# Three output products moved from the last steps of an attention kernel into its closing chain

## The chip, the cores and the metric

The kernel runs on one core of a Trainium2 chip. The metric is the device time of one execution in microseconds (us); the number of record is the median of several executions. The engines are named as in the profile: PE is TensorE (matmuls, with its weight loads listed apart as PEld), DVE is VectorE, ACT is ScalarE, POOL is GpSimd, and SP is SyncE, whose queue issues nearly all transfers (DMAs).

## What is computed

Two branches over the same `x` of 2048 tokens and 512 features are mixed by a gate:

```
g = sigmoid((x * gate_w).sum(-1))
a = softmax(q k^T / 4) v, 32 heads of 16, then @ wo      # q, k, v from x @ wqkv
b = x, with two routed tokens (the top 2 of x @ w_r) updated by a SwiGLU FFN
out = g * a + (1 - g) * b
```

## The kernel before

**Units and steps.** The attention is cut into 32 units; a unit is a pair of heads over half the queries, and the last four units (28 to 31) each take four heads over a quarter of the queries. A unit has 16 steps, one for each tile of 128 keys, so there are 512 steps. In a step `s`, `s_piece` (L634) makes four score tiles of 128x512 on PE (L641) and ACT takes their exponentials (L642) into `P`. Three of the four score tiles come from the PSUM pool `st` (3 buffers), and near the end one comes from `mxb` (1 buffer). `av_mm` (L644, L650) multiplies the exponentials with `V`, which has a column of ones, so that the sums of the softmax come out with the output; it runs two steps behind the scores. While units are left, a third stream, `m_piece` (L563, L573, L577), finds row maxima on PE and DVE; it has ended by the stretch that matters here.

**The order is written by hand.** The Python program's order is each engine's order. In the last steps a step is: four score matmuls, then `p_v(s - 2)` (the sums of two steps earlier), then one piece of the generator `slots()` (L800), then what `at_step` has registered for the step.

**The output projection.** `acc` holds 16 tiles of 128 tokens by 512 features, preloaded with `(1 - g) * b`. The features of heads 0 to 23 are projected through `wo` earlier, by `wo_part` and `acc_add` (L458: ACT scales the PSUM tile by `g` into a new tile `w`, L461, and POOL adds it to `acc`, L462). The last eight heads (feature group 3) come at the end: `split_last` (L528) splits a quarter of the queries into a rounded high part and a low rest, and `wo_last(t, 128)` (L551) does tile `t`: three matmuls (high x high, low x high, high x low; L495, in the PSUM tile `fl`), `finish` (L544: one DVE instruction, L546, `acc + g * product`) and `store` (L548, a DMA of 256 KB on SP's queue, L549). `slots()` places these for `t` = 0 to 11, one in each step: 0 to 3 from step 478 on, 4 to 7 from step 494 on, 8 to 11 from step 505 on (L846 to L850). Tiles 9, 10 and 11 therefore stand in steps 506, 507 and 508. The split halves that they read, `lastp[1]`, have been written by then.

**The closing chain.** Tiles 12 to 15 need the last unit, so they come in `tail()` (L733) after the last step, as a chain: ACT copies the sums out of PSUM (L663); PE picks the softmax sums (L739); DVE takes reciprocals (L741); ACT and DVE spread them (L744, L745); PE transposes the spread (L748) into `mxb` and `fl`; DVE multiplies (L751); ACT and DVE split into high and low (L69, L70); PE makes the four output products, three matmuls each (L758); DVE finishes each (L546) and SP stores it (L549).

## Time and profile before

| | us |
|---|---|
| median of 3 runs | 1437.01 (1435.02 to 1437.27) |
| time of the profiled execution | 1437.04 |
| its span, first to last instruction | 1435.2 |
| PE / DVE / ACT / POOL busy in the span | 1423.6 / 1295.4 / 1169.7 / 312.0 |

In the views of the profile, an entry of the timeline gives its start in the span, its length, the engine, the line and what is written from what; `x3` merges three instructions. Matmuls overlap their successors, so the length of one contains some of the next. The table by stretches of time gives for each engine the busy time and in brackets the number of instructions, and then the clock granted to TensorE as a share of full speed, the mean busy share of the 16 DMA engines (it can come out a little over 1) and GB/s. The chain of waits is followed back from the last instruction.

### The profile page before, as it was taken

What the parts mean: (1) busy time and instruction counts of PE and PEld (TensorE: products, weight loads), DVE (VectorE), ACT (ScalarE), POOL (GpSimd) and SP (SyncE); (2) the same over time, 40 slices, a digit from 0 to 9 for tenths busy, and PEclk for the clock granted to TensorE, in tenths of its full rate; (3) what the DMA queues carried; (4) which work ended last, traced back from release to release, by engine and by line L of the source; (5) the groups of instructions that cost most, each with busy time, mean ns of one, the idle gap of its engine ahead of it and who ended that gap; (6) DMA issues with size and microseconds to landing.
All of it is one profiled execution on the core that took longest, in us unless ns stands there. A gap on an engine that the chain in (4) does not pass through costs nothing.

```text
span 1435.2 us, 24154 instructions
## 1 busy us (share of the span) xinstructions
PE 1423.6 (99%) x9113; PEld 630.2 (44%) x9113; DVE 1295.4 (90%) x1535; ACT 1169.7 (82%) x2262; POOL 312.0 (22%) x328
## 2 busy tenths in 40 slices
PE   9999999999999999999999999999999999999998
PEld 6654444444444444444444444344444444444433
DVE  5879999999999999999999999999999999999942
ACT  4568888888888888888888888888888888888885
POOL 3652000112000001200000100032742322234500
PEclk9999999999999999999999999999999999999998
DMA  8612021212214121312222332414313031012012
GB/s 266 185 33 63 20 53 31 53 45 40 54 50 112 62 53 30 68 29 57 65 82 53 87 87 73 108 41 128 82 31 68 23 75 37 13 30 58 16 50 77
DMA packets 55096, 92.87 MB, mean 65 GB/s; under 512 B 14208, under 2 KB 25472, under 8 KB 53476
## 3 DMA queue, kind: packets, MB, share of 16 engines
q1 hardware_dynamic: 54884, 91.32, 24.3%
q8 instruction: 72, 1.18, 0.4%
q14 instruction: 44, 0.36, 0.1%
q0 software_dynamic: 96, 0.01, 0.0%
HBM read 63.77 MB, written 28.57 MB: 64 GB/s over the span
## 4 chain that ended last, share of the span: by engine, by line
PE 96%; DMA 2%; DVE 1%; ACT 0%; SPq 0%; issue 0%; ACTq 0%; DVEq 0%
PE av L650 35%; PE st L641 23%; PE mxa L573 12%; PE mxb L573 10%; PE fl L153 6%; PE fl L495 4%; PE st L282 3%; DMA xs<-xT 1%; PE mxa L600 1%; DMA wvs<-wqkv 1%; PE fl L386 0%; PE st L153 0%; DVE Mr L577 0%; DMA k_scr<-Qx 0%; ACT P L642 0%; PE fl L424 0%
## 5 line engine op out<-in xcount | busy, mean ns | idle before, releaser
L642 ACT ACTIVATE P<-st 128x512 f32<-128x512 f32 x2028 | 1064.5, 599 | 204.2 <-PE st L641 102.3
L577 DVE TENSOR_REDUCE Mr<-mxa 128x2 f32<-128x1024 f32 x655 | 794.4, 1213 | 4.0 <-PE mxa L573 3.5
L650 PE MATMUL av<-P,V 128*32 128x512 f32 x4096 | 545.3, 604 | 0.0
L641 PE MATMUL st<-Qx,Kx 50*128 50x512 f32 x2028 | 537.8, 443 | 1.8 <-ACT P L642 1.7
L577 DVE TENSOR_REDUCE Mr<-mxb 128x1 f32<-128x512 f32 x654 | 451.8, 691 | 63.5 <-PE st L641 18.6
L641 PEld LDWEIGHTS st<-Qx,Kx 50*128 50x128 f32 x2028 | 275.3, 184 | 232.7 <-ACT P L642 213.0
L573 PE MATMUL mxb<-Kx,Qx 48*128 48x512 f32 x654 | 325.4, 498 | 0.0
L573 PE MATMUL mxa<-Kx,Qx 48*128 48x512 f32 x1310 | 296.9, 420 | 1.2 <-DVE Mr L577 1.2
L573 PEld LDWEIGHTS mxb<-Kx,Qx 48*128 48x128 f32 x654 | 119.5, 183 | 273.7 <-DVE Mr L577 251.9
L573 PEld LDWEIGHTS mxa<-Kx,Qx 48*128 48x128 f32 x1310 | 124.9, 183 | 52.1 <-DVE Mr L577 9.9
L650 PEld LDWEIGHTS av<-P,V 128*32 128x32 f32 x4096 | 81.1, 108 | 140.6 <-issue 134.5
L189 POOL TENSOR_SCALAR ev<-pe 128x512 fp32r<-128x512 f32 x24 | 35.7, 1489 | 321.5 <-ACT pe L187 321.5
L76 POOL TENSOR_SCALAR hl<-m 128x16 fp32r<-128x16 f32 x32 | 8.1, 254 | 440.0 <-DVE m L616 440.0
L462 POOL TENSOR_TENSOR acc<-acc,w 128x512 f32<-128x512 f32 x32 | 41.0, 1280 | 166.9 <-ACT w L461 152.8
L153 PE MATMUL fl<-xh,wh 128*128 128x512 f32 x96 | 42.9, 447 | 0.0
L153 PE MATMUL fl<-xh,wl 128*128 128x512 f32 x96 | 40.4, 420 | 0.0
L546 DVE SCALAR_TENSOR_TENSOR acc<-fl,gg,acc 128x512 f32<-128x512 f32 x16 | 12.0, 748 | 26.3 <-PE fl L495 24.0
L495 PE MATMUL fl<-woh,ahl 128*128 128x512 f32 x96 | 35.2, 447 | 0.0
L605 DVE TENSOR_REDUCE Mr<-mxa 128x2 f32<-128x1024 f32 x21 | 25.7, 1222 | 8.3 <-PE mxa L600 8.3
L153 PE MATMUL fl<-xl,wh 128*128 128x512 f32 x96 | 32.6, 421 | 0.0
L190 POOL TENSOR_TENSOR ev<-pe,ev 128x512 fp32r<-128x512 f32 x24 | 30.8, 1283 | 2.0
L282 PE MATMUL st<-Kx,xh 128*128 128x512 f32 x64 | 28.1, 440 | 0.0
(173 smaller groups left out, 763.0 us busy)
## 6 DMA issues: line engine op xcount, KB each, us to landing
Kx<-k_scr SPq DMA_DIRECT2D x30, 256.0 KB
k_scr<-ev SPq DMA_DIRECT2D x14, 512.0 KB
q_scr<-ev SPq DMA_DIRECT2D x14, 512.0 KB
Qx<-q_scr SPq DMA_DIRECT2D x54, 128.0 KB
Qx<-q_scr SPq DMA_DIRECT2D x70, 64.0 KB
xs<-xT SPq DMA_DIRECT2D x16, 256.0 KB
xn<-x SPq DMA_DIRECT2D x4, 1024.0 KB
Qx<-hr SPq DMA_DIRECT2D x256, 2.0 KB
```

The costliest lines, as they stand in the source:

```text
L153: nc.tensor.matmul(ps, a[:, i, c, :], b[nb][:, c, :], start=n == 0, stop=n == 11)
L189: nc.gpsimd.tensor_scalar(ev[:, 0], t, 1.0, None, op0=OP.mult)
L190: nc.gpsimd.tensor_sub(ev[:, 1], t, ev[:, 0].bitcast(F32))
L282: nc.tensor.matmul(ps, a[nb][:, c, sl], b[:, c, :], start=c == 0 and n == 0, stop=c == 3 and n == 2)
L462: nc.gpsimd.tensor_add(a, a, w)
L495: nc.tensor.matmul(ps, a[:, sl], b[:a.shape[0], c, :], start=first and n == 0, stop=last and n == 2)
L573: nc.tensor.matmul(dst, Qx[u % 3][64 * j:64 * j + 48, t * 128:t * 128 + 128], k_of(u, t // 4)[64 * j:64 * j + 48, c * 512:c * 512 + 512], ...
L577: nc.vector.tensor_reduce(Mr[:, g0:g0 + (2 if r == 1 else 1)], MX[r - 1], axis=AX.X, op=OP.max, negate=True)
L605: nc.vector.tensor_reduce(*r, axis=AX.X, op=OP.max, negate=True)
L641: nc.tensor.matmul(ps, k, q, start=True, stop=True)
L642: nc.scalar.activation(P[s][:, 2 * j + c, :], ps, AF.Exp)
L650: nc.tensor.matmul(AV[0][32 * ct:32 * ct + 32, :], V[:, kt, h * VW:h * VW + 32], P[s][:, ct, :], start=kt == 0, stop=kt == KT - 1)
```

## The change

The loop in `slots()` now ends with tile 8, so steps 506, 507 and 508 no longer have an output product. Tiles 9, 10 and 11 are done in `tail()` by a new helper `late_wo(i)`, which makes the same three matmuls for tile 10 (`i` = 0), 11 (1) and 9 (2), into the two banks of `mxa` and into a tile of `st`. Tile 10 stands ahead of the pick of the sums and keeps its finish on DVE. Tile 11 stands after the spreading of the reciprocals, tile 9 after the split; both are finished by `acc_add`, on ACT and POOL. Each store follows its finish in SP's queue. The second bank of the last four products is now `av` in place of `mxa`.

```diff
 def tail():
     ps = st_tile((128, 16))
+    pw = mxa_tile()
+    pw = pw[:, 0], pw[:, 1], st_tile()
+
+    def late_wo(i):
+        wo_terms(pw[i], *lastp[1], 3, slice((2 + i if i < 2 else 1) * 128, (3 + i if i < 2 else 2) * 128), True, True)
+
+    late_wo(0)
+    finish(10, pw[0])
+    store(10)
     for c in range(4):
         nc.tensor.matmul(ps[:, 4 * c:4 * c + 4], o[:, c * 128:c * 128 + 128], sel_l, start=True, stop=True)
...
     nc.scalar.activation(rx[:, 0:8], rb[:, 0:8], AF.Copy)
     nc.vector.tensor_copy(rx[:, 8:16], rb[:, 8:16])
+    late_wo(1)
+    acc_add(11, pw[1], gg)
+    store(11)
     pr = [mxb_tile((128, 256)), fl_tile((128, 256))]
...
         split(hl[0][:, sl], hl[1][:, sl], o[:, sl])
-    banks = [st_tile(), mxa_tile()[:, 0], st_tile(), mxb_tile()]
+    late_wo(2)
+    acc_add(9, pw[2], gg)
+    store(9)
+    banks = [st_tile(), av_tile(), st_tile(), mxb_tile()]
...
-        for t in range(12):
+        for t in range(9):
             if t % 4 == 0:
                 yield from wait((478, 494, 505)[t // 4])
             wo_last(t, 128)
```

## The prediction

> **What bounds the kernel now.** I read the page first, then the chain of waits, then the timeline of the last 40 us.

> ```profile
> PE 1423.6 (99%) x9113; PEld 630.2 (44%) x9113; DVE 1295.4 (90%) x1535; ACT 1169.7 (82%) x2262; POOL 312.0 (22%) x328
> PE 96%; DMA 2%; DVE 1%; ACT 0%; SPq 0%; issue 0%; ACTq 0%; DVEq 0%
> ```

> PE carries the chain nearly to the end, so the change can act in two places only: the three steps that lose work, and the closing chain, where PE waits for others. The steps, in the chain (start, length) and then in the timeline:

> ```profile
> 1410.21 0.91 PE fl L495 x3
> 1411.12 0.66 PE st L641 x3
> 1411.78 1.00 PE av L650 x8
> ```

> ```profile
> 1399.01 0.73 PE L641 MATMUL st<-Qx,Kx 50*128 50x512 f32 x3
> 1400.67 1.00 PE L641 MATMUL st<-Qx,Kx 50*128 50x512 f32 x3
> 1403.08 0.73 PE L641 MATMUL st<-Qx,Kx 50*128 50x512 f32 x3
> 1405.04 0.73 PE L495 MATMUL fl<-woh,lahl 128*128 128x512 f32 x2
> 1405.93 0.50 PE L641 MATMUL st<-Qx,Kx 50*128 50x512 f32 x2
> 1413.61 0.73 PE L641 MATMUL st<-Qx,Kx 50*128 50x512 f32 x3
> 1418.65 2.78 PE L650 MATMUL av<-P,V 128*32 128x512 f32 x24
> ```

> A step with an output product is PE end to end: 0.91 + 0.66 + 1.00 = 2.57 us. Steps 503, 504 and 505 (scores from 1399.01) had none before tile 8's product at 1405.04: 6.03 us for three, 2.01 each. There ACT shares the bound:

> ```profile
> 1399.54 1.58 ACT L642 ACTIVATE P<-st 128x512 f32<-128x512 f32 x3 [0.50 <-PE st L641]
> 1401.46 1.61 ACT L642 ACTIVATE P<-st 128x512 f32<-128x512 f32 x3
> 1402.89 0.67 ACT L642 ACTIVATE P<-mxb 128x512 f32<-128x512 f32 x1
> 1403.62 1.57 ACT L642 ACTIVATE P<-st 128x512 f32<-128x512 f32 x3
> ```

> Four exponentials took 1.92 us from 1399.54 and 2.16 from 1401.46. The sums end at E = 1418.65 + 2.78 = 1421.43. From E on:

> ```profile
> 1422.15 1.05 PE L739 MATMUL st<-cst,o 128*128 128x4 f32 x8 [0.72 <-ACT o L663]
> 1423.24 0.26 DVE L741 RECIPROCAL rl<-st 128x16 f32<-128x16 f32 x1 [8.77 <-PE st L739]
> 1423.59 0.41 ACT L744 ACTIVATE rxl<-rl 128x256 f32<-128x256 f32 x1 [1.50 <-DVE rl L741]
> 1424.06 1.22 PE L748 MATMUL mxb<-cst,rxl 128*128 128x128 f32 x4 [0.86 <-ACT rxl L744]
> 1425.08 1.06 PE L748 MATMUL fl<-cst,rxl 128*128 128x128 f32 x4
> 1425.39 0.42 DVE L751 TENSOR_TENSOR o<-o,mxb 128x256 f32<-128x256 f32 x1 [1.51 <-PE mxb L748]
> 1426.37 0.79 PE L758 MATMUL st<-wz,onh 128*128 128x512 f32 x1 [0.23 <-ACT onh L69]
> 1428.86 0.63 PE L758 MATMUL mxa<-wz,onh 128*128 128x512 f32 x1
> 1429.28 0.63 PE L758 MATMUL st<-wz,onh 128*128 128x512 f32 x1
> 1431.46 0.75 DVE L546 SCALAR_TENSOR_TENSOR acc<-mxb,gg,acc 128x512 f32<-128x512 f32 x1
> ```

> PE waits 0.72, then 0.86, then 0.23 us. Its matmuls are slow too: L758's start 0.42 us apart (1428.86, 1429.28), where L495's three take 0.91 together. The granted clock says why (third number from the right; all but the first are stretches of one width, and within the first the clock halves at 27.69):

> ```profile
> 27.50:28.00 0.50, 0.50 (x3) 0.45 (x2) 0.00 (x0) 0.00 (x0) 0.50 (x1) 0.69 1.02 221
> 24.28:27.69 3.41, 1.93 (x7) 1.03 (x7) 2.45 (x3) 1.57 (x4) 2.75 (x2) 1.00 0.89 224
> 31.10:34.51 3.41, 3.01 (x13) 1.79 (x12) 3.41 (x5) 0.60 (x1) 0.00 (x0) 1.00 0.88 227
> 1420.34:1423.75 3.41, 2.15 (x20) 1.15 (x15) 0.42 (x2) 0.75 (x2) 0.00 (x0) 1.00 0.00 0
> 1423.75:1427.16 3.41, 2.87 (x10) 2.25 (x11) 1.39 (x5) 1.09 (x3) 0.00 (x0) 0.50 0.00 0
> 1427.16:1430.57 3.41, 3.41 (x9) 2.67 (x10) 1.85 (x3) 0.00 (x0) 0.00 (x0) 0.50 0.20 76
> ```

> From 1423.75 to 1430.57 PE has half its clock, 6.82 us. The stretch before had PE busy 2.15 of 3.41 us; 1.93 of 3.41 was followed by half clock as well (from 27.69 on), 3.01 was not. At half clock, 2.87 did not bring full clock back and 3.41 did.

> **The sum, part by part.** All times below are of this execution: 1437.04 us, which is its span of 1435.2 plus 1.84, and 0.03 over the median of the runs.

> *Steps 506 to 508.* Removed: nine matmuls, three finishes, three stores. The scores of 506 start at 1405.93 as before. Steps 503 to 505 are the pattern for what follows: 1405.93 + 6.03 = 1411.96 for the scores of 509, against 1413.61. For 510 and 511 I go on with the two limits seen, PE in order and four exponentials in 1.92 to 2.16 us: 2.14 and 1.96, so scores of 511 at 1416.06, where they were at 1417.69; the last sums, 24 records, then run 1417.18 to 1419.96. Taken: E' = 1419.96, **1.47 us gained**. Bounds: 3 x (2.57 - 1.9) = 2.0 above; below, if each step took the 2.41 us from 1400.67 to 1403.08, 3 x 0.16 = 0.5.

> *Tile 10*, ahead of L739. Its matmuls need nothing of the last unit and follow the sums at once: 0 to 0.91 after E', where PE idled for 0.72. L739 starts 0.19 late; with nothing to hide in it would be 0.91. The finish on DVE (0.75) stands ahead of the reciprocal: 0.97 to 1.72, the reciprocal is due at 1.81 + 0.19 = 2.00, so 0.28 of cover is left. Cost 0.19.

> *Tile 11*, after the spread. PE waited 0.86 there; the product takes 0.91 and L748 starts at 2.86 after E' (2.63 before): total lateness 0.23. The finish:

> ```profile
> L461 ACT ACTIVATE w<-fl,gg x32: 681/702/704, 1006.5 to 1363.9; 128x512 f32<-128x512 f32 x32
> L462 POOL TENSOR_TENSOR acc<-acc,w x32: 1273/1280/1292, 1007.3 to 1364.6; 128x512 f32<-128x512 f32 x32
> L70 DVE TENSOR_TENSOR wvl<-wvs,Kx x2: 681/1100/1518, 24.5 to 25.4; 128x512 fp32r<-128x512 f32 x2
> L400 PE MATMUL fl<-cst,gate x4: 272/273/321, 887.2 to 887.5; 128*112 128x128 f32 x4
> L549 SPq DMA_DIRECT2D out<-acc x16: 332/332/512, 1382.0 to 1432.2; - x16
> ```

> ACT 2.93 to 3.63, before its high split at about 4.1: hidden. POOL 3.70 to 4.98.

> *The clock.* PE's idle spots after E' shrink to about 0.1 us each, so each 3.41 us stretch has PE busy over 3.2, more than the 3.01 that kept full clock. I take full clock to the end. L748's first four then take about 0.6 in place of 1.22 (L400's four of the same size start within 0.3 us), the multiply starts at 3.6 (3.96 before) and the high split ends at 4.5 and 4.95.

> [...]

> *POOL against DVE.* L70's subtraction of two SBUF tiles took 0.68 alone and 1.52 beside POOL's own subtraction: a loss between 0 and 0.84. The first low split is due at 4.5, inside POOL's add for tile 11 (to 4.98). I take that it waits out the add, 5.0 to 5.4, and the second ends at 5.8.

> [...]

> *Tile 9*, ahead of L758. L748 now ends at 3.95, the product runs to 4.86, and L758, due at 4.5 otherwise, starts at 4.86 (4.94 before): 0.36 lost out of what the clock gave. ACT scales it behind the two high splits, 4.95 to 5.65, with nothing queued after it; POOL adds, (behind the second low split) from about 5.8 to 7.1. L758's second matmul waits for the low split to 5.45; the four products leave at full clock, three in 0.7 to 0.9, so DVE's four finishes (0.75) run back to back: 6.15 to 9.2, against 10.78 before.

> *Stores.* Each is one transfer of 256 KB, and SP's queue is in order: tile 9's store waits for POOL to 7.1, and those of 12 to 15 stand behind it (an issue is 0.33 to 0.51).

> ```profile
> 1415.50:1416.00 0.50, 0.50 (x3) 0.18 (x1) 0.00 (x0) 0.50 (x2) 0.00 (x0) 1.00 0.99 377
> 1433.00:1433.50 0.50, 0.00 (x0) 0.00 (x0) 0.00 (x0) 0.00 (x0) 0.00 (x0) 1.00 0.94 361
> 1433.50:1434.00 0.50, 0.00 (x0) 0.00 (x0) 0.00 (x0) 0.00 (x0) 0.00 (x0) 0.98 0.58 225
> ```

> At 377 GB/s a store takes 0.69 us of all 16 DMA engines. The last one before was over at about 1433.8, 1.4 ahead of the span's end; it began 0.69 earlier, at 1433.1, which is 0.85 after it was ready (1431.46 + 0.75, and 0.04 for the issue). Five stores from 7.15 on: 7.15 + 0.85 + 5 x 0.69 = 11.45, + 1.4 = 12.85 after E'. Before it was 1435.2 - 1421.43 = 13.77. **Gain 0.92**; without this queue it would be 9.2 + 2.99 = 12.19, a gain of 1.6.

> Sum: 1437.04 - 1.47 - 0.92 = **1434.65**, so 1434.6.

> **The rivals.**

> 1. *The stores don't queue* (POOL early, or data flowing sooner): the end is DVE's. 1.6 to 1.95 in the chain (the latter without the wait on POOL) with 1.47: 1433.6 to 1434.0, say 1433.8. For it: in the main sum the queue costs only 0.7. Against: 377 GB/s looks like a ceiling.

> 2. *The clock falls once, later.* L739 is counted as busy but moves four columns; should it weigh nothing, the emptiest stretch has about 2.2 of 3.41, near the 2.15 that halved the clock. With the boundary where it was, 1423.75 = E' + 3.8, tile 9's product ends at 5.4 and the finishes at 9.9 (full clock back at 7.2; stores then end at 13.35) or 11.4 (at 10.6; 14.4): 1435.1 to 1436.2.

> 3. *The steps don't shrink*, because ACT's ring holds them at 2.41: 0.5 in place of 1.47, 1435.6.

> 4. *Slower: the inserted products run at half clock.* If a stretch that closes right after L739, at E' + 2.0, is judged too empty and the next two are as well, tile 11 takes 1.3, L748 2.1, tile 9 1.3 and the twelve matmuls of L758 5.1 us, one after the other from 2.0 on: 11.8, last finish 12.6, end 15.6, which is 1.83 over 13.77. Less 1.47: 1437.4. It decides the sign only if the fall comes before about E' + 3 and the low clock lasts 6.8 us, as it did before. Against it: two such stretches would be filled with products.

> **The chances.** Main sum 0.46, rival 1 0.20, rival 2 0.21, rival 3 0.06, rival 4 0.07. About 0.2% (2.9 us) can be told from no change here, so faster means below 1434.1: nearly all of rival 1 and about a third of the main sum, whose terms carry about half a microsecond, 0.33. Slower, over 1439.9, needs rival 4 with the low splits each losing their 0.84 on top and more: 0.03. The rest, 0.64, is within. The range leaves out rival 4 and the lower edge of rival 1: 1433.2 to 1436.5.

> **What would show it.** Steps 506 to 511 at about 2.0 us with the sums ending near 1420.0; L739 0.9 after the sums; the reciprocal not waiting for L546; granted clock 1.00 from there to the last matmul, with L758's starts 0.23 apart; the first low split waiting for L462; the store of tile 9 last to become ready and those of 12 to 14 issued right behind it; DMA engines full for over 3 us at the end. The prediction is wrong if the clock still falls before L758, if finish 10 holds the reciprocal, or if the last sums don't move.

## The result and the profile after

| | before | changed |
|---|---|---|
| median of 22 runs each, us | 1436.79 | 1434.67 |
| profiled execution, us (span) | 1437.04 (1435.2) | 1434.91 (1433.1) |
| scores of step 506 to the end of the sums, us | 15.50 | 14.00 |
| end of the sums to the end of the span, us | 13.77 | 12.39 |

The ratio of the times is 0.9984, with a 95% interval of 0.9978 to 0.9990: 2.3 us less, between 1.4 and 3.2. One of the 22 runs of before took 1798.27 us; without it the median of before is 1436.70. The predicted 1434.6 holds. The interval does not reach zero gain, but the gain lies within the 0.2% that the prediction called no clear change.

The two lower rows are read from the timeline. First the steps of the changed kernel (start, length, instruction):

```profile
1406.71 0.50 PE L641 MATMUL st<-Qx,Kx 50*128 50x512 f32 x2
1417.93 2.78 PE L650 MATMUL av<-P,V 128*32 128x512 f32 x24
```

The sums end at 1417.93 + 2.78 = 1420.71, 14.00 us after the scores of 506. These scores themselves start 0.78 us later than in the profile of before (1405.93), ahead of anything that was changed. So the two spans differ by 2.1 us, while the changed part alone gained 1.50 + 1.38 = 2.88. One place where such shifts can arise is seen in e1, below.

Then the closing chain, from the same view; L748, L750, L760 and L773 are what were L739, L741, L748 and L758:

```profile
1420.64 0.73 PE L495 MATMUL mxa<-woh,lahl 128*128 128x512 f32 x2
1421.44 1.04 PE L748 MATMUL st<-cst,o 128*128 128x4 f32 x8
1422.52 0.26 DVE L750 RECIPROCAL rl<-st 128x16 f32<-128x16 f32 x1
1423.34 0.71 PE L760 MATMUL mxb<-cst,rxl 128*128 128x128 f32 x4
1424.26 1.28 POOL L462 TENSOR_TENSOR acc<-acc,w 128x512 f32<-128x512 f32 x1 [18.98 <-ACT w L461]
1425.13 1.04 DVE L70 TENSOR_TENSOR onl<-o,onh 128x256 fp32r<-128x256 f32 x2 [0.17 <-ACT onh L69]
1425.15 0.50 PE L773 MATMUL st<-wz,onh 128*128 128x512 f32 x1
1425.89 0.50 PE L773 MATMUL st<-wz,onl 128*128 128x512 f32 x1 [0.23 <-DVE onl L70]
1426.07 1.29 POOL L462 TENSOR_TENSOR acc<-acc,w 128x512 f32<-128x512 f32 x1 [0.52 <-ACT w L461]
1428.76 0.75 DVE L546 SCALAR_TENSOR_TENSOR acc<-mxb,gg,acc 128x512 f32<-128x512 f32 x1
```

Read the starts against the end of the sums: the pick at 0.73 (0.72 before), the reciprocal at 1.81 (1.81), L760 at 2.63 (2.63). The two inserted products cost nothing. L760 then takes 0.71 in place of 1.22, and the last finish ends at 1429.51, 8.80 after the sums in place of 10.78. The two low splits (L70) take 1.04 us from the start of the first to the end of the second (0.70 and 0.41 each); before it was 0.99, but there each took 0.42, with a gap between them. The second matmul of L773 waits for the first of them. Last the stretches: PE's busy time is the second number, the granted clock the third from the right, then the busy share of the DMA engines:

```profile
1418.57:1421.98 3.41, 3.41 (x28) 1.52 (x20) 0.34 (x1) 1.45 (x3) 0.00 (x0) 1.00 0.00 0
1421.98:1425.39 3.41, 3.41 (x20) 2.47 (x19) 2.02 (x6) 1.81 (x5) 1.13 (x1) 1.00 0.20 77
1425.39:1428.81 3.42, 3.10 (x12) 1.99 (x11) 2.92 (x6) 0.60 (x2) 1.44 (x2) 1.00 0.38 144
1428.00:1431.70 3.70, 0.72 (x4) 0.24 (x2) 1.51 (x3) 0.00 (x0) 0.00 (x0) 1.00 0.94 354
```

From 1418.57 on the clock is full as long as there are matmuls, with PE busy 3.10 us or more of each 3.41. From 1428.00 to 1431.70 the 16 DMA engines are busy for 0.94 of 3.70 us, 3.48 us: five stores at 0.70. They end the chain now, as e4 and e5 show below.

### The profile page after: what moved, and what is told of

It is laid out like the page before. It is cut to its first block, busy times and chain, and to the rows that moved or that the text cites. A ratio compares the mean times of both kernels' runs of the same rounds, so it can differ in the third digit from the quotient of the medians.

```text
span 1433.1 us, 24158 instructions
## 1 busy us (share of the span) xinstructions
PE 1420.6 (99%) x9113; PEld 628.1 (44%) x9113; DVE 1294.0 (90%) x1533; ACT 1170.6 (82%) x2264; POOL 314.8 (22%) x330
## 4 chain that ended last, share of the span: by engine, by line
PE 96%; DMA 1%; DVE 1%; SPq 1%; ACT 0%; issue 0%; DVEq 0%; ACTq 0%
PE av L650 36%; PE st L641 23%; PE mxa L573 12%; PE mxb L573 10%; PE fl L153 6%; PE fl L495 4%; PE st L282 3%; DMA xs<-xT 1%; PE mxa L600 1%; DMA wvs<-wqkv 1%; PE fl L386 0%; PE st L153 0%; DVE Mr L577 0%; ACT P L642 0%; PE fl L424 0%; PE mxb L641 0%
## 5 line engine op out<-in xcount | busy, mean ns | idle before, releaser
L642 ACT ACTIVATE P<-st 128x512 f32<-128x512 f32 x2028 | 1064.6, 599 | 202.4 <-PE st L641 107.8
L650 PE MATMUL av<-P,V 128*32 128x512 f32 x4096 | 545.3, 604 | 0.0
L641 PE MATMUL st<-Qx,Kx 50*128 50x512 f32 x2028 | 537.5, 443 | 1.8 <-ACT P L642 1.8
L641 PEld LDWEIGHTS st<-Qx,Kx 50*128 50x128 f32 x2028 | 275.5, 184 | 234.0 <-ACT P L642 215.5
L650 PEld LDWEIGHTS av<-P,V 128*32 128x32 f32 x4096 | 81.1, 108 | 140.1 <-issue 134.0
L462 POOL TENSOR_TENSOR acc<-acc,w 128x512 f32<-128x512 f32 x34 | 43.5, 1280 | 186.8 <-ACT w L461 172.6
L495 PE MATMUL fl<-woh,ahl 128*128 128x512 f32 x96 | 35.2, 447 | 0.0
L546 DVE SCALAR_TENSOR_TENSOR acc<-fl,gg,acc 128x512 f32<-128x512 f32 x13 | 9.7, 748 | 20.7 <-PE fl L495 18.5
```

What stands on the lines that cost most here:

```text
L462: nc.gpsimd.tensor_add(a, a, w)
L495: nc.tensor.matmul(ps, a[:, sl], b[:a.shape[0], c, :], start=first and n == 0, stop=last and n == 2)
L641: nc.tensor.matmul(ps, k, q, start=True, stop=True)
L642: nc.scalar.activation(P[s][:, 2 * j + c, :], ps, AF.Exp)
L650: nc.tensor.matmul(AV[0][32 * ct:32 * ct + 32, :], V[:, kt, h * VW:h * VW + 32], P[s][:, ct, :], start=kt == 0, stop=kt == KT - 1)
```

## The experiments

Each kernel is read by the same two lengths, the only ones that the change touches; a profile is one execution. "Steps" is from the scores of 506 to the end of the sums, "chain" from there to the end of the span.

| kernel | steps | chain | median us (runs) | ratio to before, 95% interval |
|---|---|---|---|---|
| before | 15.50 | 13.77 | | |
| changed | 14.00 | 12.39 | 1434.67 (22) | 0.9984 (0.9978 to 0.9990) |
| e1_steps_only | 14.01 | 13.97 | 1435.66 (11) | 0.9991 (0.9982 to 1.0000) |
| e2_fill_only | 15.50 | 11.54 | 1435.74 (11) | 0.9992 (0.9983 to 1.0001) |
| e3_store9_last | 14.01 | 12.55 | 1434.63 (11) | 0.9988 (0.9979 to 0.9997) |
| e4_no_store9 | 14.01 | 11.83 | 1434.60 (11) | 0.9983 (0.9974 to 0.9992) |
| e5_dve_finish11 | 14.01 | 12.41 | 1434.25 (11) | 0.9981 (0.9972 to 0.9990) |
| e6_two_moved | 14.46 | 11.58 | 1433.62 (11) | 0.9983 (0.9974 to 0.9992) |
| e7_one_fill | 15.51 | 11.54 | 1434.72 (10) | 0.9987 (0.9977 to 0.9996) |
| e9_two_moved_lead_fill | 14.45 | 11.56 | 1433.35 (9) | 0.9977 (0.9967 to 0.9987) |
| e10_before_again | 15.50 | 13.69 | 1436.62 (1) | |
| e11_one_matmul | 15.51 | 14.03 | 1437.97 (1) | |
| e12_after_again | 14.02 | 12.45 | 1434.79 (11) | 0.9987 (0.9978 to 0.9996) |
| e13_two_moved_again | 14.45 | 11.54 | 1433.75 (11) | 0.9984 (0.9975 to 0.9993) |

The lengths of one kernel repeat within 0.1 us where it was profiled twice, the times of executions spread over 2 to 5 us. Differences of half a microsecond are therefore read from the lengths, and the medians say only whether they contradict. The median of before, timed beside the experiments, was 1436.46 to 1436.75.

**The steps alone.** The loop ends with tile 8 and nothing is added:

```diff
-        for t in range(12):
+        for t in range(9):
             if t % 4 == 0:
```

> Leaves out the products, finishes and stores of tiles 9, 10 and 11 altogether; the closing chain is that of the kernel before. My theory (two separate gains: steps about 1.5 us, closing chain about 1.4 us through the clock): from the scores of step 506 to the end of the sums 14.0 us where it was 15.50, the granted clock halves in the closing chain again, which stays about 13.8 us from the end of the sums to the end of the span; about 1.5 us faster than before. Rival (the steps give all of it, the chain nothing): 2.1 to 2.9 us faster. Rival (ACT holds the steps): sums end less than 0.6 us earlier.

The sums of e1, and PE's stretches behind them:

```profile
1409.52 0.50 PE L641 MATMUL st<-Qx,Kx 50*128 50x512 f32 x2
1420.75 2.78 PE L650 MATMUL av<-P,V 128*32 128x512 f32 x24
```

```profile
1422.36:1425.77 3.41, 2.23 (x20) 1.15 (x15) 0.34 (x2) 0.67 (x2) 0.00 (x0) 1.00 0.00 0
1425.77:1429.18 3.41, 2.79 (x10) 2.16 (x10) 1.39 (x4) 1.17 (x3) 0.00 (x0) 0.50 0.00 0
```

14.01 us for the steps, and a chain of 13.97 that runs at half clock for 6.83 us, as my theory had it; ACT does not hold the steps, and the chain's gain is not a by-product of shorter steps. The median is 1.0 us below that of before.

This execution also began its step 506 at 1409.52, 3.6 us later than the profile of before. The clock had halved near the start, where PE waits for a DMA and for DVE:

```profile
29.77:33.18 3.41, 1.41 (x8) 0.83 (x7) 1.94 (x3) 1.14 (x2) 0.00 (x0) 0.99 0.62 177
33.18:36.60 3.42, 3.42 (x9) 2.49 (x10) 3.40 (x5) 0.00 (x0) 0.00 (x0) 0.50 0.88 217
36.60:40.01 3.41, 3.41 (x10) 2.18 (x11) 0.00 (x0) 0.05 (x1) 0.00 (x0) 0.51 0.91 183
```

PE was busy 1.41 of 3.41 us, and half clock followed, here from 33.13 to 39.96; in the profile of before it was 27.69 to 31.10. PE had idled there for 2.43 us (for a DMA) and 2.00 us (for DVE), 1.48 and 0.40 in before. These longer waits and the longer half clock could make up the 3.6 us; that they do was not shown, and how much of the spread of all executions comes from this place was not measured.

**The filling alone.** The twelve products stay in the steps, and the three of the closing chain are made besides, their result unused:

```diff
         late_wo(0)
-        finish(10, pw[0])
-        store(10)
...
-        for t in range(9):
+        for t in range(12):
```

(likewise without what follows `late_wo(1)` and `late_wo(2)`)

> All twelve products stay in the steps as before; the three products of late_wo are made once more in the closing chain, and their result is not used (no finish, no store, no POOL). My theory (the products keep PE's clock up): steps as before (15.5 us from the scores of 506 to the end of the sums), granted clock 1.00 through the chain, last finish at about 8.5 us after the sums in place of 10.78, and, without a fifth store in the queue, an end at about 11.5 us in place of 13.77: 2.3 us faster than before with nine matmuls more. Rival (inserted work lengthens a chain that is bound by its waits): chain 13.8 us or longer, no faster or slower by up to 1 us.

The sums, the low splits and the last finish of e2, and its stretches:

```profile
1405.76 0.50 PE L641 MATMUL st<-Qx,Kx 50*128 50x512 f32 x2
1418.48 2.78 PE L650 MATMUL av<-P,V 128*32 128x512 f32 x24
1425.67 0.76 DVE L70 TENSOR_TENSOR onl<-o,onh 128x256 fp32r<-128x256 f32 x2 [0.16 <-ACT onh L69]
1428.97 0.75 DVE L546 SCALAR_TENSOR_TENSOR acc<-mxb,gg,acc 128x512 f32<-128x512 f32 x1
```

```profile
1420.96:1424.37 3.41, 3.35 (x22) 2.34 (x19) 0.55 (x2) 1.01 (x2) 0.00 (x0) 1.00 0.00 0
1424.37:1427.79 3.42, 3.42 (x18) 2.47 (x17) 2.43 (x6) 0.75 (x2) 0.00 (x0) 1.00 0.00 0
```

Nine matmuls more, and the chain is 2.23 us shorter (11.54), with the steps as before. The chain's gain is the clock's alone: no work has left it. (The bank `av` in place of `mxa` came along in e2, as in e7 and e11; it is not the cause, since e11, below, has it too and a chain of 14.03.) The changed kernel's chain is 0.85 longer than this one, which is the price of finishing and storing three tiles there. The median fell by 0.9 us only, where the profile gives 2.2; the interval reaches from 2.4 us gained to none. So it does not contradict the profile, but does not confirm its size either.

**The price of the fifth store.** In e3 tile 9's store comes last, in e4 it is left out:

```diff
         acc_add(9, pw[2], gg)
-        store(9)
...
             store(12 + t)
+        store(9)
```

The last line is e3's alone.

> The changed kernel with the store of tile 9 put behind that of tile 15 in SP's queue. Theory A (the five last stores are bound by the transfers' own rate, 0.69 us each): chain 12.4 us as in the changed kernel, within 0.2. Theory B (the prediction's wording: SP's queue waits in order for POOL's add of tile 9, and what stands behind it is late): the stores of 12 to 14 leave 0.3 to 0.7 us earlier and the chain ends up to 0.5 us earlier.

> The changed kernel without the store of tile 9 (its rows of the output are not written). Both theories of the store queue: the chain ends at 8.80 + 2.99 = 11.8 us after the sums in place of 12.4, 0.6 us faster than the changed kernel. If neither holds and DVE's finishes end the chain in any case: 12.4 us as in the changed kernel.

The end of the sums and the DMA engines (last two numbers: busy share, GB/s) over the last stores, of e3 and then of e4:

```profile
1416.27 2.78 PE L650 MATMUL av<-P,V 128*32 128x512 f32 x24
1426.50:1430.20 3.70, 0.56 (x3) 0.12 (x1) 1.35 (x2) 0.00 (x0) 0.00 (x0) 1.00 0.95 354
```

```profile
1418.59 2.78 PE L650 MATMUL av<-P,V 128*32 128x512 f32 x24
1428.90:1431.80 2.90, 0.44 (x2) 0.01 (x1) 1.23 (x2) 0.00 (x0) 0.00 (x0) 1.00 0.97 362
```

e3 moves five stores in 0.95 x 3.70 = 3.5 us and its chain is 12.55; e4 moves four in 2.8 us and its chain is 11.83. So the fifth store costs 0.56 us against the changed kernel and 0.72 against e3, and moving it to the end gains nothing: the transfers' rate is the limit (theory A). The prediction had about this price, but named SP's order as a cause beside the rate; tile 9's add ends at 6.65 after the sums in the changed kernel and the first of the others' finishes at 6.71, so the order holds nobody up here. Whether an add that ended later would do so was not shown.

**ACT and POOL as finishers.** Tile 11 finished on DVE:

```diff
         late_wo(1)
-        acc_add(11, pw[1], gg)
+        finish(11, pw[1])
```

> The changed kernel with tile 11 finished by one DVE instruction in place of ACT and POOL. Theory A (the first low split waits out POOL's add of tile 11, and the queue of five stores ends the chain): the two low splits take 0.76 us together in place of 1.04, L758's second matmul starts 0.25 us earlier, and the chain still ends at 12.2 to 12.4 us after the sums, because tile 9's add on POOL and the five transfers stay. Rival (the low splits are slowed by something else): 1.04 us as in the changed kernel. Rival (DVE's finishes end the chain): 0.3 us shorter. Against it: the finish may hold DVE's first multiply, due at 3.45 after the sums, by 0.1 us.

```profile
1416.81 2.78 PE L650 MATMUL av<-P,V 128*32 128x512 f32 x24
1423.99 0.76 DVE L70 TENSOR_TENSOR onl<-o,onh 128x256 fp32r<-128x256 f32 x2 [0.15 <-ACT onh L69]
1424.47 0.50 PE L773 MATMUL st<-wz,onl 128*128 128x512 f32 x1
```

The low splits take 0.76, as in e2 where POOL is idle too, against 1.04 beside POOL's add; the second matmul starts 4.88 after the sums in place of 5.18. The first low split of the changed kernel starts 4.42 after the sums and POOL's add ends at 4.83, so the split loses 0.28 of the 0.41 us for which the add still ran. The profile of before points the same way: there a subtraction of L70 on DVE took 1.52 us beside POOL's own, and 0.68 where POOL's began 0.42 us after it. By itself e5 does not tell POOL from ACT, whose scaling of tile 11 goes with the add. The chain is 12.41 all the same, although DVE's last finish ends 0.32 us earlier (8.48 after the sums), because five stores end it.

**Two tiles in place of three.** What e4 and e5 show points to a version that leaves tile 9 in its step and finishes both others on DVE:

```diff
-        acc_add(11, pw[1], gg)
+        finish(11, pw[1])
...
-        late_wo(2)
-        acc_add(9, pw[2], gg)
-        store(9)
...
-        for t in range(9):
+        for t in range(10):
```

> Only tiles 10 and 11 are moved, both finished on DVE; tile 9 stays in step 506. My theory: the steps give 1.0 in place of 1.5 us (14.5 us from the scores of 506 to the end of the sums), but nothing is left in the queue ahead of the stores of 12 to 15 and no POOL add beside the low splits: chain 11.4 to 11.5 us in place of 12.39, if the clock holds. Together 0.4 us better than the changed kernel, 3.3 better than before. Rival: with tile 9's product gone from ahead of L758, PE is idle for 0.5 us more and the clock falls: chain 12.5 us or longer.

> The changed kernel once more, side by side with e13_two_moved_again. If its chain is set by the clock kept up and the five stores, the chain is 12.4 us from the end of the sums again and 14.0 us lie between the scores of 506 and the end of the sums, wherever the stretches of the clock fall; about 1434.5 us.

> e6_two_moved once more, on the chip of e12_after_again. By the chains seen (14.46 + 11.58 against 14.0 + 12.4) it is 0.35 us faster than the changed kernel, 1434.1; by the medians of the first call it would be 1.0 faster. If its emptiest stretch, PE busy about 2.8 of 3.41 us, falls worse against the stretches of the clock, the clock halves and the chain is over 12.5 us.

```profile
1406.56 0.50 PE L641 MATMUL st<-Qx,Kx 50*128 50x512 f32 x2
1418.24 2.78 PE L650 MATMUL av<-P,V 128*32 128x512 f32 x24
1428.77 0.75 DVE L546 SCALAR_TENSOR_TENSOR acc<-mxb,gg,acc 128x512 f32<-128x512 f32 x1
```

```profile
1422.42:1425.83 3.41, 2.78 (x16) 1.92 (x15) 2.74 (x8) 1.16 (x3) 0.00 (x0) 1.00 0.33 127
1425.83:1429.25 3.42, 2.90 (x12) 1.99 (x11) 2.92 (x6) 0.00 (x0) 0.00 (x0) 1.00 0.34 128
```

The steps give up 0.45 us and the chain wins 0.8 (11.58, and 11.54 in e13): 26.0 us together, where the changed kernel has 26.4 and the kernel before 29.3. Timed side by side (e13 and e12), the medians are 1433.75 and 1434.79; those of e6 and of the changed kernel, which were not timed side by side, are 1.05 apart as well. The lengths explain 0.4 of that; the intervals of the two ratios overlap, so that e6 is the faster of the two is likely, and its size is open.

**How much filling the clock needs.** From e2, e7 keeps only the product ahead of the pick (unused), e11 only the first matmul of it, e10 is the kernel before:

```diff
         late_wo(0)
...
-        late_wo(1)
...
-        late_wo(2)
```

> As e2_fill_only, with the product ahead of the pick alone (once more, result unused); the other two are left out. It asks how much filling the clock needs: PE is then idle for 0.86 us ahead of L748 and 0.5 us ahead of L758. If a stretch with PE busy about 2.6 of 3.41 us is enough: clock 1.00 and a chain of 11.5 us. If it is not: the clock halves and the chain is 12.5 to 14 us. The stretches seen so far leave 2.15 (it fell) to 3.01 (it held) open.

> As e7_one_fill, with a single matmul (result unused) ahead of the pick in place of three: PE idle for about 0.45, 0.86 and 0.6 us in the chain. If the clock goes by PE's busy time in its stretch and the limit lies between 2.15 us (fell) and 2.55 us (held, e7_one_fill): a stretch of about 2.3 to 2.5 us, near the limit. Held: chain 11.5 us. Fell: 12.5 to 14 us. Either outcome narrows the limit or moves it.

> The kernel before, unchanged, profiled once more. Theory (the clock is judged in stretches of 3.41 us whose place against the kernel differs from execution to execution): the clock halves in the closing chain again, at a moment that lies elsewhere against the end of the sums, so that the chain is 12.3 to 14 us; from the scores of 506 to the end of the sums 15.5 us as ever. Rival (the place is fixed against the kernel): the clock halves 2.3 us after the end of the sums and the chain is 13.8 us again.

The stretches of e7, of e11 and of e10 that decide, each cut where the clock's own stretches lie in that execution (counted in steps of 3.4133 us from its fall near the start):

```profile
1422.42:1425.83 3.41, 2.55 (x20) 1.50 (x12) 0.55 (x2) 1.01 (x2) 0.00 (x0) 1.00 0.00 0
1425.83:1429.24 3.41, 2.78 (x14) 2.12 (x15) 1.98 (x5) 0.75 (x2) 0.00 (x0) 1.00 0.00 0
```

```profile
1421.47:1424.88 3.41, 2.26 (x18) 1.24 (x10) 0.55 (x2) 1.01 (x2) 0.00 (x0) 1.00 0.00 0
1424.88:1428.29 3.41, 3.18 (x11) 2.46 (x12) 1.60 (x4) 0.83 (x2) 0.00 (x0) 0.50 0.00 0
```

```profile
1419.78:1423.19 3.41, 2.38 (x24) 1.15 (x15) 0.26 (x1) 0.78 (x2) 0.00 (x0) 1.00 0.00 0
1423.19:1426.60 3.41, 2.63 (x9) 2.07 (x9) 1.46 (x4) 1.12 (x3) 0.00 (x0) 0.50 0.00 0
```

In the closing chain, half clock followed stretches with PE busy 2.15 (before), 2.23 (e1), 2.26 (e11) and 2.38 us (e10); full clock stayed after 2.55 (e7), 2.78, 2.90, 3.10 and more. So one product was enough in this execution of e7, and one matmul was not in that of e11.

But PE's busy time is not all that the clock goes by. Cut along the clock's own stretches in the same way, the parts near the start of e7 and of the changed kernel read:

```profile
22.95:26.36 3.41, 1.75 (x8) 0.94 (x6) 2.53 (x4) 3.16 (x6) 1.06 (x1) 1.00 0.84 213
26.36:29.78 3.42, 2.89 (x11) 2.13 (x12) 0.87 (x1) 0.00 (x0) 2.02 (x2) 1.00 0.87 220
```

```profile
29.34:32.76 3.42, 3.12 (x8) 1.92 (x6) 1.58 (x2) 0.86 (x2) 0.00 (x0) 0.50 0.59 165
32.76:36.17 3.41, 3.12 (x13) 2.21 (x14) 3.41 (x6) 0.34 (x1) 0.00 (x0) 1.00 0.89 222
```

In e7 a stretch with PE busy 1.75 kept full clock. So did two stretches near the start of e1, with 1.99 and 2.42 us, while others there, with 1.41 (e1) to 2.25 us (e9), were followed by half clock. Coming back is no clearer: 2.63 (e10), 2.70 (e6), 2.79 (e1), 2.87 (before) and 3.18 us (e11) at half clock were not enough, nor was one full stretch in e1 (33.18, above), but 3.12 was in the changed kernel. What else counts stays open; of the stretches given here, the fullest that lost full clock had 2.38 us (e10).

In e10 the clock halves 2.08 us after the sums, in before 2.31, in e11 2.71: the stretches lie differently in each execution, and the profiles of before, e1, e10 and e11 have chains of 13.7 to 14.0. Not every execution of before can look like this. Its two half clocks, 3.41 and 6.83 us, make a mean granted clock of 0.996, and 42 of its 85 runs beside the experiments have that. But 34 have 0.998, which leaves at most 7.2 us at half clock (0.0025 x 2 x 1435), and 4 have 0.999. In these a fall was missing or shorter. The runs with 0.998 were 0.6 to 1.9 us faster in the mean than those with 0.996, which may be why the medians gain less than the lengths.

The chain of e7, 11.54, is that of e2. But PE idles 0.86 and 0.63 us in it, and a stretch that held both would have it busy for about 1.9 us only. Of its ten runs, five have a mean granted clock of 0.999 or 1.000, at most 4.3 us at half clock, which leaves no room for a fall of 6.8 us; the other five, with 0.998, leave it open. The chain of the changed kernel has no stretch below 3.1 as long as matmuls are left, that of e6 none below about 2.75, wherever the stretches lie.

**The other fall, near the start.** e6 with ten unused matmuls where PE waits between 24 and 34 us (`busy(n)` makes `n` matmuls into a tile of `st`):

```diff
+            if (n, i) in ((0, 1), (1, 0)):
+                busy(7 if n == 0 else 3)
             if i == 0:
                 tl = mxa_tile()
```

> e6_two_moved with ten more matmuls whose result is unused, near the start, where PE waits for a DMA (seven, 1.6 us) and for DVE (three, 0.7 us) between 24 and 34 us and the clock halves for 3.4 to 6.8 us in the runs seen. If idle time there is what halves the clock: granted clock 1.00 from 20 to 40 us, 1 to 3 us faster than e6_two_moved, and a narrower spread of its runs. Rival (the lead is bound by DVE and the transfers, not by PE's clock): no change, or up to 0.7 us slower.

```profile
24.00:27.00 3.00, 3.00 (x14) 1.79 (x12) 2.84 (x4) 2.06 (x4) 1.85 (x2) 1.00 0.83 208
27.00:29.25 2.25, 1.09 (x3) 0.52 (x4) 0.12 (x1) 0.00 (x0) 1.24 (x1) 1.00 0.78 172
25.91:29.32 3.41, 2.25 (x9) 1.24 (x8) 1.21 (x1) 0.15 (x1) 2.33 (x2) 1.00 0.77 208
29.33:32.74 3.41, 3.41 (x10) 2.64 (x9) 2.27 (x3) 0.60 (x1) 0.00 (x0) 0.50 0.85 215
```

In this execution the filling is full (3.00 of 3.00), but behind it PE waits for the next transfer instead (1.16 us; busy 1.09 of 2.25, and 2.25 in the clock's own stretch from 25.91), so the clock halves at 29.32. Other executions went better: six of the nine have a mean granted clock of 1.000, at most 1.4 us at half clock, so there the clock did not fall near the start: in every profile that fall lasts 3.41 us or more. e6 has two of eleven with 1.000, e13 one. Yet the median lies only 0.27 us below e6's, and the spread of the runs is no narrower (2.1 us, e6 2.0). So the forecast missed: the 1 to 3 us for keeping the clock near the start were not seen. This favours the rival, that the start is bound by other things, but 0.27 us is too little to tell from none.

## Why the prediction was right

**Steps 506 to 508: right.** 1.47 was taken from the pattern of steps 503 to 505, 1.50 came out, and e1 shows the same with nothing else changed. The steps on the way agree too: the scores of 511 start 10.12 us after those of 506 (1416.83), 10.13 were forecast.

**Tiles 10 and 11: the cost was over-sized.** The prediction let each product hold PE for 0.91 us, from its first start to its last end, and had the pick 0.19 and L760 0.23 us late. Both start on time. The product ahead of the pick starts at 1420.64 and the pick at 1421.44, 0.80 later, as soon as its operand is there: the last of the 0.91 overlaps with what follows. A gap of 0.72 plus the product's early start, right behind the last sums, was room enough.

**The clock: right, and it is what pays.** The tail's stretches hold PE busy for 3.10 us or more, the granted clock stays at 1.00, and e2 and e7 show that the products pay by being made and not by being taken from elsewhere. The prediction took it that stretches busier than 3.01 us are safe, and no stretch given here contradicts that; but busy time as the only measure was an assumption, and the stretches near the start speak against it (1.75 us kept full clock in e7). The stretches given here that half clock followed were not idle ones: PE was busy 1.41 (e1) to 2.38 us (e10) of each 3.41.

**POOL against DVE: right in kind, over-sized.** The prediction let the first low split wait from 4.5 to 5.0 for the end of POOL's add and had the second end at 5.8. It lost 0.28 us, and the second ended at 5.46.

**Tile 9: late start over-sized.** L773 starts 4.44 after the sums, not 4.86; 0.23 of the difference is the lateness that didn't come, and the rest is L760, shorter than forecast; together they let the product start at 3.55 in place of 3.95.

**Stores: right in price, half right in reason.** 0.66 was forecast for the queue of five (12.85 less 12.19), 0.56 measured (e4). It comes from the rate of the transfers (354 GB/s over the last stores, their engines busy for 0.94 of 3.70 us); SP's order, which the prediction named as well, has no part in it (e3). POOL's add for tile 9 ended at 6.65, ahead of the first of the other finishes, and not at 7.1, behind it. The last packet ended 1.3 us ahead of the span's end, where 1.4 was taken.

**The sum.** 2.39 us was forecast, 2.88 came out of the two lengths, and the difference is for the most part the 0.42 us that L773 and tile 9's product start earlier than forecast, carried to the stores. That the time on record lies within 0.1 us of the forecast is partly luck: the medians moved by 2.1 us where the lengths say 2.88, and what happens ahead of step 506 moves single executions by more than the gain (its scores start between 1405.0 and 1409.5 us in the profiles). Of the rivals, none came: the stores do queue, the clock did not fall in any of the six profiles with all three products in the chain, ACT did not hold the steps.

## What to carry to other kernels

Here a chain of short dependent stages at the end of a kernel ran at half the matmul clock for 6.83 of its 13.77 us, although PE looked mostly busy (2.15 of 3.41 us in the stretch ahead of the fall, 2.87 in the next); in another kernel, look at the granted clock there before counting instructions. Work that PE must do anyway, put into the gaps of that chain, was worth more than its own time: the steps became 1.50 us shorter without it and the chain 1.38 us shorter with it, and in the profile of e7 a single group of three matmuls was enough (chain 11.54 us). But finishing and storing that work there filled the queue of last transfers, 0.56 to 0.72 us for the fifth store (e4 against the changed kernel and e3): move as many tiles as the gaps hide, and not one more.
